# Decode attention with a gated FFN: TensorE's twelve looped rounds as one nest of two loops, with the FFN's transposes behind it

## The chip, the cores and the metric

The kernel runs on one core of one Trainium2 chip. A time is device microseconds of one execution; the median of a few executions is what counts. The engines are named as in the profile: PE (TensorE; PEld is its weight load), DVE (VectorE), ACT (ScalarE), POOL (GpSimd) and SP (SyncE, which here only issues DMAs).

## The reference

Two inputs of 448 numbers (batch B = 2, one token) go through an attention block with a cache of 4096 keys and values for each of 16 heads (width 256), and through a feed-forward net (FFN); a gate mixes the two. All is float32.

```python
g = sigmoid((x * gate_w).sum(-1, keepdims=True))
q = (x @ wq).reshape(B, 1, 16, 256).transpose(0, 2, 1, 3)
scores = einsum("bhqd,bhkd->bhqk", q, k_cache) * 256 ** -0.5
o = einsum("bhqk,bhkd->bhqd", softmax(scores), v_cache)
a = o.transpose(0, 2, 1, 3).reshape(B, 1, 4096) @ wo
h = x @ w1 + b1                  # 448 -> 1792
b = (max(h, 0) ** 2) @ w2 + b2   # 1792 -> 448
out = g * a + (1 - g) * b
```

The two caches are 268 MB of the 290 MB that the kernel reads.

## The kernel before, in words

**Rounds.** The work is cut into 16 rounds. A round is one batch row and two heads: 8.39 MB of keys and 8.39 MB of values. The two heads lie on partitions 0 to 63 and 64 to 127, 64 cache rows of 256 numbers on each partition. Keys have two buffers (`kp[0]`, `kp[1]`, even and odd rounds), values have one (`vp`).

**One round.** DVE multiplies the keys with q, spread over all partitions, and adds up each product row: `times_q` and `row_sums` for one half of the buffer, then the other (together `rest`). `maximum` takes the largest score of each partition on DVE and lets PE turn these into rows (tile `mt`); `softmax` takes the negative maximum of a head on DVE (`nb`) and the exponentials and their sums on ACT (`pw`, `rs`). `values` multiplies `pw` with the values, 32 matmuls on PE into the PSUM bank `po`. `make_q` spreads the q of a later round with a matmul of one picked column (`sel`, written by `pick` on ACT).

**Groups.** Four heads (two batch rows, so four rounds) are a group u. After the fourth round `sums(u)` adds the exponentials' sums over partitions, `norm(u)` makes the factors on DVE, `turn_wide(u)` copies `po` to `shared` on ACT and transposes and scales it on PE, and `project(u)` multiplies it with this group's rows of `wo` into `acc`. Rounds 0 to 11 (`LOOPED`) are groups 0 to 2; the last four rounds have code of their own, with w2 loaded last of all.

**The FFN.** x times w1 goes into the PSUM bank `ph` early on. ACT copies it to `h_sb` (in `shared`), `ffn_turn` transposes it with 28 small matmuls between round 0's softmax and the loops, and `ffn_square` (five DVE instructions: bias, maximum with 0, square, gate) stands on DVE between round 1's `rest` and its `maximum`. Its result `hT` is first used with w2, at the end.

**Order.** Every engine executes its instructions in the order in which the program calls `op`. `Flow.op` works out the semaphore waits from the regions that an instruction reads and writes. SP issues all large loads on one DMA queue, in program order, and each waits for its buffer to come free: `load_k(i + 2)` for `row_sums` of round i, `load_v(i + 1)` for `values` of round i. On PE the four rounds of a group are a loop of the hardware (`Fori`), with the group's end as straight code behind it, three times over. In such a loop waits have to be the same on each pass, so they are tokens: a semaphore that an instruction of another engine raises (`give`) and PE lowers again (`take`).

Of the kernel before, what the change touches and what calls it, by code (L numbers as in the profile page):

```python
# [23 lines left out]
class Flow:  # L24
# [7 lines left out]
    def __init__(self, nc):  # L32
        self.nc = nc
        self.eng = {PE: nc.tensor, ACT: nc.scalar, DVE: nc.vector, POOL: nc.gpsimd, SP: nc.sync}
        self.order = {e: [] for e in self.eng}
        self.ops = {}
        self.know = {e: {} for e in self.eng}
        self.seen = {}
        self.tokens = {}
        self.body, self.at, self.passes = None, 0, 0  # L40

# [4 lines left out]
    def op(self, eng, fn, r=(), w=(), give=None, take=(), dma=None):  # L46
        proc = dma or eng
        looped = eng == PE and self.body is not None
        o = Op(proc, eng, fn, give, looped)
# [38 lines left out]
        if looped:  # L88
            if self.passes == 1:
                self.body.append(o)  # L90
            else:
                first = self.body[self.at]
# [11 lines left out]

    def loop(self):
        self.body, self.passes = [], 0

    def next_pass(self):
        assert self.passes < 2 or self.at == len(self.body)
        self.passes += 1  # L110
        self.at = 0

    def end_loop(self, slot=None):
        assert self.at == len(self.body)
        self.order[PE].append((self.passes, self.body, slot))
        self.body = None

    def emit(self):
# [36 lines left out]
        for eng in (POOL, DVE, ACT, SP, PE):  # L155
            for o in self.order[eng]:
                if isinstance(o, Op):
                    one(o)
                else:
                    passes, body, slot = o  # L160
                    with nc.Fori(0, passes, engines=bass.OrderedEngineSet([TYPES[PE]]),
                                 head_slot=None if slot is None else {TYPES[PE]: slot}):
                        for p in body:
                            one(p)
            if eng == SP:
                nums = sorted(s.num for s in sems.values())
                assert nums == list(range(nums[0], nums[0] + len(nums)))
                nc.sync.sem_clear(range(nums[0], nums[0] + len(nums)))


def gated_mix_kernel(nc, x, k_cache, v_cache, wq, wo, w1, b1, w2, b2, gate_w, out):
# [134 lines left out]
    def vec(fn, r, w, give=None):  # L306
# [12 lines left out]
    vec(lambda: v_.tensor_reduce(m16, ident.rearrange("p (r k) -> p k r", r=4)[:, :4 * HG, :], axis=AX.X, op=ALU.add),  # L319
        ["ident"], ["m16"])  # L320

    xr = start_at[:, 4 * D:].rearrange("b (k r s) -> b k r s", k=XC, s=2)
# [51 lines left out]
    def make_q(i, token=False):  # L374
        c = sel if token else col(i)
        op(PE, mms([(pq[k * PH:(k + 1) * PH, :DH], c.to_broadcast([P, PH]), qs[:, k * DH:(k + 1) * DH], True, True)
                    for k in range(2)]), r=["qs", "sel" if token else "ident"], w=["pq"], take=["q"] if token else ())
        t = q_t[i % 3]
        q_of[i] = t
        op(ACT, lambda: s_.activation(t, pq[:, :DH], AF.Copy), r=["pq"], w=[f"q{i % 3}"])  # L380

    def pick(i):
        c = col(i)
        op(ACT, lambda: s_.activation(sel, c, AF.Copy), r=["ident"], w=["sel"], give="q")

# [6 lines left out]

    h_sb = shared[:2 * B, :F // 2]
    op(PE, times_x(ph, w1_t, D, FB // 2), r=["xT", place(vp, 0, D * F // P)], w=["ph"])
    for k in range(FB // 2):
        op(ACT, lambda k=k: s_.activation(h_sb[:, k * D:(k + 1) * D], ph[32 * k:32 * k + 2 * B, :D], AF.Copy),
           r=["ph"], w=[("shared", k * D, (k + 1) * D)])
    load_k(1)
# [20 lines left out]
    def maximum(i, token=False):  # L419
        s = s_t[i % 2]  # L420
        vec(lambda: v_.tensor_reduce(m, s, axis=AX.X, op=ALU.max), [f"s{i % 2}"], ["m"], give="m" if token else None)
        op(PE, mms([(mt[k * PH:(k + 1) * PH, :PH], m.to_broadcast([P, PH]), ident[:, k * PH:(k + 1) * PH], True, True)
                    for k in range(2)]), r=["m", "ident"], w=["mt"], take=["m"] if token else ())

# [3 lines left out]
    def softmax(i):  # L428
        b, n = rounds[i]
        s, nb, rs, pw = s_t[i % 2], nb_t[i % 2], None, pwt[buf(i)]  # L430
        vec(lambda: v_.tensor_reduce(nb, mt[:, :PH], axis=AX.X, op=ALU.max, negate=True), ["mt"], [f"nb{i % 2}"])  # L431
        u, k = unit_of[2 * n]
        rs = rs_t[u % 2]

        def part(e):
            at = slice(e * PH, (e + 1) * PH)
            c = B * (k + e) + b
            op(ACT, lambda: s_.activation(pw[at, :, 2 * c:2 * c + 2], s[at].rearrange("p (m s) -> p m s", s=2), AF.Exp,  # L438
                                          bias=nb[at], accum_out=rs[at, c:c + 1]),
               r=[f"s{i % 2}", f"nb{i % 2}"], w=[(f"pw{buf(i)}", 2 * c, 2 * c + 2), (f"rs{u % 2}", c, c + 1)],  # L440
               give="pw" if e and i < LOOPED else None)

        part(0)
        part(1)

    def clear(i):
# [4 lines left out]
           w=[("pw0", 2 * (B * (k + e) + b), 2 * (B * (k + e) + b) + 2) for e in range(2)])  # L451

    def sums(u):
        n = B * len(units[u])
        op(PE, mms([(sm[:, :n], ones_pp, rs_t[u % 2][:, :n], True, True)]), r=["ones", f"rs{u % 2}"], w=["sm"])

# [23 lines left out]

    o_w = shared.rearrange("r (s j k p) -> r s j k p", s=2, j=HJ // 2, k=HG)

    def turn_wide(u):
        ptv = sm[:, :HJ * HG * B].rearrange("p (j c) -> p j c", c=HG * B)
        po, rl = po_t[0], rl_t[u % 2]
        pv = po.rearrange("r (s p j) -> r s j p", s=2, j=HJ)
        for lo in range(0, HJ, HJ // 2):
            for s in range(2):
                op(ACT, lambda s=s, lo=lo: s_.activation(o_w[:, s], pv[:, s, lo:lo + HJ // 2].unsqueeze(2).to_broadcast([P, HJ // 2, HG, HP]),  # L489
                                              AF.Copy), r=["po0"], w=[("shared", s * HN // 2, (s + 1) * HN // 2)])  # L490
            ov = o_w.rearrange("r s j k p -> r s j (k p)")
            op(PE, mms([(ptv[:, lo + j, :], ov[:, s, j, :], rl[:, :, s], s == 0, s == 1)
                        for j in range(HJ // 2) for s in range(2)]), r=["shared", f"rl{u % 2}"], w=["sm"])
        if u < NG - 2:
            op(ACT, lambda: s_.activation(po, zero.to_broadcast([P, 512]), AF.Copy), r=["zero"], w=["po0"])
        for k in range(HG):
            at = slice(k * HP, (k + 1) * HP)
            op(ACT, lambda k=k, at=at: s_.activation(oTw[at], ptv[at, :, B * k:B * k + B], AF.Copy), r=["sm"], w=[("oTw", k, k + 1)])  # L498

# [15 lines left out]
    def load_wo(u):  # L515
        if u < NG - 1:
            load(SP, "wo", wo_t, wo_g[u], ["wo"])
        else:
            load(SP, "wo", wo_t.rearrange("p (h k) -> p h k", h=HG), wo_v[:, u * HG:(u + 1) * HG, :], ["wo"])

    def project(u):
        t = wo_t.rearrange("p (j n) -> p j n", j=HJ)
        op(PE, mms([(acc[:B, :D], oTw[:, j, :], t[:, j, :], False, u == NG - 2 and j == HJ - 1) for j in range(HJ)]),
           r=["oTw", "wo"], w=["acc"])

# [42 lines left out]
    softmax(0)  # L568
    pt = ffn_turn()
    make_q(2)  # L570
    pick(3)

    for i in range(LOOPED):
        if i % HG == 0:
            flow.loop()
        flow.next_pass()
        vt = load_v(i, vp)
# [9 lines left out]
        softmax(i + 1)  # L587
        make_q(i + 3, True)
# [101 lines left out]
```

## Time and profile before

| | |
|---|---|
| median of 3 runs | 677.68 us (677.60 to 677.97) |
| the profiled execution | 677.82 us, its span 676.5 us |
| DVE busy | 570.2 us, 84% |
| PE busy | 245.4 us, 36% |
| ACT busy | 42.3 us, 6% |
| read from HBM | 289.56 MB, 428 GB/s over the span |
| share of the 16 DMA engines, SP's queue | 99.3% |

The page lists busy time by engine, 40 equal slices of the span, the DMA queues, and the chain of work that ended last. The timeline lists instructions by their start in us from the span's start. In both, a row of a group gives out<-in by tile name, the shape, the count, busy us and mean ns of one, and behind the bar the idle time before it and what ended it. PE executes each float32 matmul as two, so 32 matmuls of the program are x64 in the trace. The DMA rows count KB of 1024 bytes.

### The profile page before, as it was taken

What the parts mean: (1) busy time and instruction counts of PE and PEld (TensorE: products, weight loads), DVE (VectorE), ACT (ScalarE), POOL (GpSimd) and SP (SyncE); (2) the same over time, 40 slices, a digit from 0 to 9 for tenths busy, and PEclk for the clock granted to TensorE, in tenths of its full rate; (3) what the DMA queues carried; (4) which work ended last, traced back from release to release, by engine and by line L of the source; (5) the groups of instructions that cost most, each with busy time, mean ns of one, the idle gap of its engine ahead of it and who ended that gap; (6) DMA issues with size and microseconds to landing.
All of it is one profiled execution on the core that took longest, in us unless ns stands there. A gap on an engine that the chain in (4) does not pass through costs nothing.

```text
span 676.5 us, 3789 instructions
## 1 busy us (share of the span) xinstructions
PE 245.4 (36%) x1658; PEld 83.3 (12%) x1658; DVE 570.2 (84%) x143; ACT 42.3 (6%) x141; POOL 0.7 (0%) x6
## 2 busy tenths in 40 slices
PE   2522350502305761140505456050411580412476
PEld 1100210100001410010101411010100140100122
DVE  3069999999999895979979896897979899999920
ACT  0001000010100201010000201000010110000000
POOL 0000000000000000000000000000000000000000
PEclk9957585655758577585756678575665765675889
DMA  9999999999999999999999999999999999999997
GB/s 381 426 438 435 435 434 434 434 434 434 434 434 434 419 435 434 434 434 434 434 434 434 457 431 434 434 434 434 430 434 430 401 460 434 434 434 434 392 439 304
DMA packets 7062, 289.71 MB, mean 428 GB/s; under 512 B 902, under 2 KB 1036, under 8 KB 1932
## 3 DMA queue, kind: packets, MB, share of 16 engines
q1 hardware_dynamic: 6880, 289.54, 99.3%
q8 instruction: 8, 0.13, 0.1%
q10 hardware_dynamic: 172, 0.02, 0.0%
q14 instruction: 2, 0.02, 0.0%
HBM read 289.56 MB, written 0.01 MB: 428 GB/s over the span
## 4 chain that ended last, share of the span: by engine, by line
DMA 48%; DVE 31%; PE 3%; SPq 1%; issue 0%; DVEq 0%
DMA kp<-in_A_k_cache_dram 32%; DVE s L409 15%; DVE kp L404 15%; DMA vp<-in_A_v_cache_dram 11%; DMA kp<-in_B_w_dram 5%; PE po L333 3%; SPq L254 1%; PE fin L333 0%; PE mt L333 0%; DVE shared L660 0%; DVEq L147 0%; DVE nb L431 0%
## 5 line engine op out<-in xcount | busy, mean ns | idle before, releaser
L404 DVE TENSOR_TENSOR kp<-kp,q 128x8192 f32<-128x8192 f32 (+2 forms) x34 | 278.2, 8183 | 57.6 <-DMA kp<-in_A_k_cache_dram 57.6
L409 DVE TENSOR_REDUCE s<-kp 128x32 f32<-128x8192 f32 x32 | 278.0, 8686 | 1.1
L333 PE MATMUL po<-vp,pw 128*16 128x512 f32 (+1 forms) x960 | 135.8, 728 | 233.0 <-PEq L145 208.9
L333 PEld LDWEIGHTS po<-vp,pw 128*16 128x16 f32 (+1 forms) x960 | 31.1, 110 | 333.5 <-issue 307.3
L333 PE MATMUL mt<-ident,m 128*64 128x64 f32 x64 | 7.3, 318 | 141.3 <-PEq L145 87.4
L333 PE MATMUL sm<-rl,shared 128*128 128x8 f32 (+1 forms) x112 | 23.6, 347 | 9.2 <-ACT shared L489 8.1
L333 PE MATMUL acc<-wo,oTw 128*2 128x448 f32 x48 | 24.8, 683 | 2.5 <-ACT oTw L498 2.5
L333 PEld LDWEIGHTS sm<-rl,shared 128*128 128x128 f32 x112 | 23.0, 311 | 10.8 <-DVE rl L462 4.6
L450 ACT ACTIVATE pw<-zero 128x128 f32<-128x128 f32 x12 | 3.7, 312 | 325.5 <-PE po L333 325.5
L333 PEld LDWEIGHTS mt<-ident,m 128*64 128x64 f32 x64 | 4.8, 191 | 155.0 <-issue 99.0
L438 ACT ACTIVATE pw<-s,nb 64x64 f32<-64x64 f32 x32 | 11.1, 348 | 169.8 <-DVE nb L431 169.6
L660 DVE COPY shared<-fin 128x112 f32<-128x112 f32 x1 | 0.3, 275 | 20.8 <-PE fin L333 20.8
L333 PE MATMUL ph<-vp,xT 128*4 128x448 f32 x28 | 8.2, 759 | 15.6 <-DMA vp<-in_B_w_dram 15.6
L333 PE MATMUL po<-kp,pw 128*8 128x512 f32 x64 | 9.4, 744 | 8.8 <-DMA kp<-in_A_v_cache_dram 8.8
L333 PE MATMUL pq<-qs,sel 128*64 128x256 f32 x48 | 12.3, 594 | 0.0
L431 DVE TENSOR_REDUCE nb<-mt 128x1 f32<-128x64 f32 x16 | 3.6, 224 | 9.8 <-PE mt L333 9.8
L333 PE MATMUL po<-vp,xT 128*4 128x512 f32 x56 | 8.7, 787 | 4.9 <-DMA vp<-in_A_wq_dram 4.9
L460 DVE RECIPROCAL rc<-sm 128x8 f32<-128x8 f32 (+1 forms) x5 | 1.0, 196 | 7.7 <-PE sm L333 7.7
L380 ACT ACTIVATE q<-pq 128x256 f32<-128x256 f32 x16 | 6.1, 383 | 21.0 <-PE pq L333 20.7
L489 ACT ACTIVATE shared<-po 128x512 f32<-128x512 f32 x12 | 6.5, 591 | 11.4 <-PE sm L333 11.4
L333 PEld LDWEIGHTS acc<-wo,oTw 128*2 128x2 f32 x48 | 4.5, 98 | 20.6 <-issue 17.8
L438 ACT ACTIVATION_READ_ACCUMULATOR pw<-s,nb 64x1 f32 x32 | 5.9, 184 | 0.0
(65 smaller groups left out, 66.2 us busy)
## 6 DMA issues: line engine op xcount, KB each, us to landing
vp<-in_A_wq_dram SPq DMA_DIRECT2D x1, 7168.0 KB, 19.4
wo<-in_A_wo_dram SPq DMA_DIRECT2D x4, 1792.0 KB, 45.2
vp<-in_A_v_cache_dram SPq DMA_DIRECT2D x1, 4096.0 KB, 24.8
vp<-in_B_w_dram SPq DMA_DIRECT2D x1, 3136.0 KB, 18.0
vp<-in_A_v_cache_dram SPq DMA_DIRECT2D x1, 3072.0 KB, 31.7
kp<-in_B_w_dram SPq DMA_DIRECT2D x1, 1344.0 KB, 37.1
vp<-in_A_v_cache_dram SPq DMA_DIRECT2D x1, 1024.0 KB, 33.7
kp<-in_B_w_dram SPq DMA_DIRECT2D x2, 448.0 KB, 33.5
```

What stands on the lines that cost most here:

```text
L254: op(eng, lambda: e.dma_start(dst, src), r=r, w=w, dma=sem, give=give)
L333: i = t_.matmul(out_, lhsT, rhs, start=start, stop=stop, skip_group_check=True)
L380: op(ACT, lambda: s_.activation(t, pq[:, :DH], AF.Copy), r=["pq"], w=[f"q{i % 3}"])
L404: vec(lambda: v_.tensor_tensor(kt, kt, q.unsqueeze(1).to_broadcast([P, hi - lo, DH]), op=ALU.mult), at + [f"q{i % 3}"], at)
L409: vec(lambda: v_.tensor_reduce(s[:, at], rows(t)[:, at, :], axis=AX.X, op=ALU.add), [place(t, half * HALF, (half + 1) * HALF)], [(f"s{i % ...
L431: vec(lambda: v_.tensor_reduce(nb, mt[:, :PH], axis=AX.X, op=ALU.max, negate=True), ["mt"], [f"nb{i % 2}"])
L438: op(ACT, lambda: s_.activation(pw[at, :, 2 * c:2 * c + 2], s[at].rearrange("p (m s) -> p m s", s=2), AF.Exp, bias=nb[at], accum_out=rs[at ...
L450: op(ACT, lambda: s_.activation(at, zero.unsqueeze(2).unsqueeze(3).to_broadcast([P, NK // 2, 2, 2]), AF.Copy), r=["zero"], w=[("pw0", 2 * ...
L460: vec(lambda: v_.reciprocal(c, sm[:, :B * n].rearrange("p (k b) -> p k b", b=B)), ["sm"], ["rc"])
L489: op(ACT, lambda s=s, lo=lo: s_.activation(o_w[:, s], pv[:, s, lo:lo + HJ // 2].unsqueeze(2).to_broadcast([P, HJ // 2, HG, HP]), AF.Copy), ...
L660: vec(lambda: v_.tensor_copy(y4, fin[:, :DQ]), ["fin"], [("shared", 0, DQ)])
```

## The change

PE's three loops of four passes become one nest: an outer loop over the groups 0 to 2, an inner loop over a group's four rounds, and the group's end (`sums`, turn, `project`) as the rest of the outer body. Waits of that rest become tokens too: `turn` and `oT` from ACT, `wo` from the load, and `pick` now gives the `pw` token that `values` takes. Some steps have fewer matmuls. `make_q` and `maximum` have one full-width matmul each in place of two half-width ones (and two half-height copies or reductions behind them). At a group's end DVE itself scales and adds the two column halves of `po` into a tile `o` of 256 columns (`norm_wide`, five instructions where `norm` had three), ACT writes it to `shared` in one instruction of 1024 columns, and PE turns it with 8 matmuls where it had 16. The sums of a group are held in a copy (`rs_w`).

The FFN's turn moves from ahead of the loops to behind them, with `ffn_square` right after it. Its input stays in the PSUM bank `ph` until then, and ACT copies it, twice over, into the tile `wo_t` after the third `project` has read that. It has 14 matmuls of 128 columns for 28 of 64.

```diff
@@ Flow.emit
+                    outer, inner, body, rest, slot = o
+                    with nc.Fori(0, outer, engines=engines, head_slot={TYPES[PE]: slot}):
+                        with nc.Fori(0, inner, engines=engines):
+                            for p in body:
+                                one(p)
+                        for p in rest:
                             one(p)
@@ make_q, pick, maximum
-        op(PE, mms([(pq[k * PH:(k + 1) * PH, :DH], c.to_broadcast([P, PH]), qs[:, k * DH:(k + 1) * DH], True, True)
-                    for k in range(2)]), r=["qs", "sel" if token else "ident"], w=["pq"], take=["q"] if token else ())
+        op(PE, mms([(pq[:, :2 * DH], c.to_broadcast([P, P]), qs, True, True)]), r=["qs", "sel" if token else "ident"], w=["pq"])
...
-        op(ACT, lambda: s_.activation(sel, c, AF.Copy), r=["ident"], w=["sel"], give="q")
+        op(ACT, lambda: s_.activation(sel, c, AF.Copy), r=["ident"], w=["sel"], give="pw")
...
+        op(PE, mms([(mt[:, :P], m.to_broadcast([P, P]), ident, True, True)]), r=["m", "ident"], w=["mt"], take=["m"] if token else ())
@@ the early copies of ph are gone
-    h_sb = shared[:2 * B, :F // 2]
-    for k in range(FB // 2):
-        op(ACT, lambda k=k: s_.activation(h_sb[:, k * D:(k + 1) * D], ph[32 * k:32 * k + 2 * B, :D], AF.Copy),
-           r=["ph"], w=[("shared", k * D, (k + 1) * D)])
@@ a group's end
+    def norm_wide(u):
+        c = rc[:, :HG]
+        po = po_t[0]
+        vec(lambda: v_.reciprocal(c, sm[:, :B * HG].rearrange("p (k b) -> p k b", b=B)), ["sm"], ["rc"])
+        vec(lambda: v_.tensor_tensor(c, c, gP[:, 0, :].unsqueeze(1).to_broadcast([P, HG, B]), op=ALU.mult), ["rc", "gP"], ["rc"])
+        vec(lambda: v_.tensor_tensor(rw, m8, c.rearrange("p k b -> p (k b)"), op=ALU.mult), ["m8", "rc"], ["rw"])
+        vec(lambda: v_.tensor_scalar(o_t, po[:, :DH], eo[:, 0:1], None, op0=ALU.mult), ["po0", "eo"], ["o"])
+        vec(lambda: v_.scalar_tensor_tensor(o_t, po[:, DH:], eo[:, 1:2], o_t, op0=ALU.mult, op1=ALU.add), ["po0", "eo", "o"], ["o"])
 
     def turn_wide(u):
...
+        op(ACT, lambda: s_.activation(o_w, o_t.rearrange("r (p j) -> r j p", j=HJ).unsqueeze(2).to_broadcast([P, HJ, HG, HP]),
+                                      AF.Copy), r=["o"], w=["shared"], give="turn")
+        ov = o_w.rearrange("r j k p -> r j (k p)")
+        op(PE, mms([(ptv[:, j, :], ov[:, j, :], rw, True, True) for j in range(HJ)]), r=["shared", "rw"], w=["sm"], take=["turn"])
@@ the FFN's turn
     def ffn_turn():
-        hv = h_sb.rearrange("r (p c) -> r c p", c=FC)
+        h_sb = wo_t[:2 * B, :F]
+        hv = h_sb.rearrange("r (a k n) -> r k a n", a=2, k=FB // 2)
+        for k in range(FB // 2):
+            op(ACT, lambda k=k: s_.activation(hv[:, k], ph[32 * k:32 * k + 2 * B, :D].unsqueeze(1).to_broadcast([2 * B, 2, D]), AF.Copy),
+               r=["ph"], w=["wo"])
+        hc = h_sb.rearrange("r (m c) -> r c m", c=FC)
         pt = sm[:, :FC * 2 * B].rearrange("p (c r) -> p c r", r=2 * B)
-        op(PE, mms([(pt[a * PH:(a + 1) * PH, c, :], hv[:, c, :], ident[:2 * B, :2 * B], True, True)
-                    for c in range(FC) for a in range(2)]), r=["shared", "ident"], w=["sm"])
+        op(PE, mms([(pt[:, c, :], hc[:, c, :], ident[:2 * B, :2 * B], True, True) for c in range(FC)]), r=["wo", "ident"], w=["sm"])
         return pt
@@ the order of the program
     softmax(0)
-    pt = ffn_turn()
     make_q(2)
     pick(3)
 
+    flow.nest()
     for i in range(LOOPED):
...
         clear(i)
         rest(i + 1, 0, 0)
-        if i == 0:
-            ffn_square(pt)
...
         if i % HG == HG - 1:
+            flow.enter("outer")
             u = i // HG
-            flow.end_loop(16 * u)
             sums(u)
-            norm(u)
+            norm_wide(u)
             turn_wide(u)
             project(u)
+    flow.end_nest(NG - 1, HG, 39)
+    pt = ffn_turn()
+    ffn_square(pt)
 
     i = last - 3
     load_k(i + 2)
```

How this moves instructions, at the places of which the prediction speaks. In the kernel before, DVE has the FFN's five instructions (L560 to L564) between the sums and the maximum of round 1:

```order
L409 TENSOR_REDUCE s1<-kp1 128x32
L560 TENSOR_TENSOR hb<-sm,b1T 64x28 x2
L562 TENSOR_SCALAR hb<-hb 128x28
L563 TENSOR_TENSOR hT<-hb 128x28
L564 TENSOR_TENSOR hT<-hT,gP 128x28
L421 TENSOR_REDUCE m<-s1 128x1
```

They read `sm`, which PE filled ahead of its loops. At the end of the third group, behind round 12's maximum (L421, L431), DVE has the factors (L460 to L462) and then round 13's keys:

```order
L421 TENSOR_REDUCE m<-s0 128x1
L431 TENSOR_REDUCE nb0<-mt 128x1
L460 RECIPROCAL rc<-sm 128x8
L461 TENSOR_TENSOR rc<-rc,gP 128x8
L462 TENSOR_TENSOR rl0<-m16,rc 128x16
```

In the changed kernel (its own line numbers) the same place on DVE holds, between round 12's maximum and round 13's keys (L412 on kp1), the factors, the two instructions that make `o`, and the FFN:

```order
L429 TENSOR_REDUCE m<-s0 128x1
L440 TENSOR_REDUCE nb0<-mt 64x1 x2
L499 RECIPROCAL rc<-sm 128x8
L500 TENSOR_TENSOR rc<-rc,gP 128x8
L501 TENSOR_TENSOR rw<-m8,rc 128x8
L502 TENSOR_SCALAR o<-po0,eo 128x256
L503 SCALAR_TENSOR_TENSOR o<-po0,eo,o 128x256
L582 TENSOR_TENSOR hb<-sm,b1T 64x28 x2
L584 TENSOR_SCALAR hb<-hb 128x28
L585 TENSOR_TENSOR hT<-hb 128x28
L586 TENSOR_TENSOR hT<-hT,gP 128x28
L412 TENSOR_TENSOR kp1<-kp1,q1 128x8192
```

So the FFN's instructions now stand ahead of round 13's products, and what they read is made on PE at that same time. PE's order there, in the changed kernel, from the head of the inner loop (L166; L165 is the outer one) to the FFN's transposes:

```order
L166 UNCONDITIONAL_BRANCH
L344 MATMUL po0<-vp,pw0 16x512 x32
L344 MATMUL mt<-ident,m 128x128
L344 MATMUL pq<-qs,sel 128x512
L166 REGISTER_ALU
L166 COMPARE_AND_BRANCH
L344 MATMUL sm<-rs_w,ones_pp 128x8
L344 MATMUL sm<-rw,shared 128x8 x8
L344 MATMUL acc<-wo,oTw 2x448 x8
L165 REGISTER_ALU
L165 COMPARE_AND_BRANCH
L344 MATMUL sm<-ident,wo 128x4 x14
```

The FFN's 14 transposes (the last row) come behind the third `project` (`acc`), where the kernel before goes from `project` straight to round 13's maximum.

More of the change, by code (lines that the diff above doesn't have):

```diff
@@ L39, in __init__ @@
         self.tokens = {}
-        self.body, self.at, self.passes = None, 0, 0
+        self.parts, self.part, self.at = None, None, 0
     @staticmethod
@@ L47, in op @@
         proc = dma or eng
-        looped = eng == PE and self.body is not None
+        looped = eng == PE and self.part is not None
         o = Op(proc, eng, fn, give, looped)
@@ L88, in op @@
         if looped:
-            if self.passes == 1:
-                self.body.append(o)
+            if self.at is None:
+                self.parts[self.part].append(o)
             else:
-                first = self.body[self.at]
+                first = self.parts[self.part][self.at]
                 assert first.takes == o.takes and not o.waits, (first.takes, o.takes)
@@ L103, in learn, with nest, enter, leave @@
         know[p.proc] = max(know.get(p.proc, 0), p.n)
[L105 to L116, printed above, removed]
+    def nest(self):
+        self.parts = {}
+    def enter(self, part):
+        self.leave()
+        self.part, self.at = part, 0 if part in self.parts else None
+        self.parts.setdefault(part, [])
+    def leave(self):
+        assert self.part is None or self.at in (None, len(self.parts[self.part]))
+        self.part = None
+    def end_nest(self, outer, inner, slot):
+        self.leave()
+        self.order[PE].append((outer, inner, self.parts["inner"], self.parts["outer"], slot))
     def emit(self):
@@ L159, in emit @@
                 else:
[L160 to L163, printed above, removed]
+                    outer, inner, body, rest, slot = o
+                    engines = bass.OrderedEngineSet([TYPES[PE]])
+                    with nc.Fori(0, outer, engines=engines, head_slot={TYPES[PE]: slot}):
[3 more added lines that the diff above has]
+                        for p in rest:
                             one(p)
@@ L220, in gated_mix_kernel @@
     m16 = sb("m16", P, 4 * HG)
+    m8 = sb("m8", P, 2 * HG)
+    rw = sb("rw", P, 2 * HG)
+    o_t = sb("o", P, DH)
+    rs_w = sb("rs_w", P, B * HG)
     xT = sb("xT", P, 2, XC, 2, B)
@@ L320, in gated_mix_kernel @@
         ["ident"], ["m16"])
+    vec(lambda: v_.tensor_reduce(m8, m16.rearrange("p (c s) -> p c s", s=2), axis=AX.X, op=ALU.add), ["m16"], ["m8"])
     xr = start_at[:, 4 * D:].rearrange("b (k r s) -> b k r s", k=XC, s=2)
@@ L375, in make_q @@
         c = sel if token else col(i)
-        op(PE, mms([(pq[k * PH:(k + 1) * PH, :DH], c.to_broadcast([P, PH]), qs[:, k * DH:(k + 1) * DH], True, True)
-                    for k in range(2)]), r=["qs", "sel" if token else "ident"], w=["pq"], take=["q"] if token else ())
+        op(PE, mms([(pq[:, :2 * DH], c.to_broadcast([P, P]), qs, True, True)]), r=["qs", "sel" if token else "ident"], w=["pq"])
         t = q_t[i % 3]
         q_of[i] = t
-        op(ACT, lambda: s_.activation(t, pq[:, :DH], AF.Copy), r=["pq"], w=[f"q{i % 3}"])
+        for k in range(2):
+            at = slice(k * PH, (k + 1) * PH)
+            op(ACT, lambda k=k, at=at: s_.activation(t[at], pq[at, k * DH:(k + 1) * DH], AF.Copy), r=["pq"], w=[(f"q{i % 3}", k, k + 1)])
     def pick(i):
         c = col(i)
-        op(ACT, lambda: s_.activation(sel, c, AF.Copy), r=["ident"], w=["sel"], give="q")
+        op(ACT, lambda: s_.activation(sel, c, AF.Copy), r=["ident"], w=["sel"], give="pw")
     op(PE, times_x(po_t[1], wq_t, QB, NQ // 2), r=["xT", place(vp, 0, D * N // P)], w=["po1"])
@@ L421, in maximum @@
         vec(lambda: v_.tensor_reduce(m, s, axis=AX.X, op=ALU.max), [f"s{i % 2}"], ["m"], give="m" if token else None)
-        op(PE, mms([(mt[k * PH:(k + 1) * PH, :PH], m.to_broadcast([P, PH]), ident[:, k * PH:(k + 1) * PH], True, True)
-                    for k in range(2)]), r=["m", "ident"], w=["mt"], take=["m"] if token else ())
+        op(PE, mms([(mt[:, :P], m.to_broadcast([P, P]), ident, True, True)]), r=["m", "ident"], w=["mt"], take=["m"] if token else ())
     def buf(i):
@@ L430, in softmax @@
         s, nb, rs, pw = s_t[i % 2], nb_t[i % 2], None, pwt[buf(i)]
-        vec(lambda: v_.tensor_reduce(nb, mt[:, :PH], axis=AX.X, op=ALU.max, negate=True), ["mt"], [f"nb{i % 2}"])
+        for k in range(2):
+            at = slice(k * PH, (k + 1) * PH)
+            vec(lambda at=at: v_.tensor_reduce(nb[at], mt[at, at], axis=AX.X, op=ALU.max, negate=True), ["mt"], [(f"nb{i % 2}", at.start, at.stop)])
         u, k = unit_of[2 * n]
-        rs = rs_t[u % 2]
+        rn = u % 2 if u > NG - 2 else 0
+        rs = rs_t[rn]
         def part(e):
@@ L439, in part @@
                                           bias=nb[at], accum_out=rs[at, c:c + 1]),
-               r=[f"s{i % 2}", f"nb{i % 2}"], w=[(f"pw{buf(i)}", 2 * c, 2 * c + 2), (f"rs{u % 2}", c, c + 1)],
-               give="pw" if e and i < LOOPED else None)
+               r=[f"s{i % 2}", (f"nb{i % 2}", e * PH, (e + 1) * PH)], w=[(f"pw{buf(i)}", 2 * c, 2 * c + 2), (f"rs{rn}", c, c + 1)])
         part(0)
@@ L451, in clear, with hold_sums @@
            w=[("pw0", 2 * (B * (k + e) + b), 2 * (B * (k + e) + b) + 2) for e in range(2)])
+    def hold_sums():
+        op(ACT, lambda: s_.activation(rs_w, rs_t[0], AF.Copy), r=["rs0"], w=["rs_w"])
     def sums(u):
         n = B * len(units[u])
-        op(PE, mms([(sm[:, :n], ones_pp, rs_t[u % 2][:, :n], True, True)]), r=["ones", f"rs{u % 2}"], w=["sm"])
+        rs, name = (rs_t[u % 2], f"rs{u % 2}") if u > NG - 2 else (rs_w, "rs_w")
+        op(PE, mms([(sm[:, :n], ones_pp, rs[:, :n], True, True)]), r=["ones", name], w=["sm"])
     def norm(u):
@@ L479, in values @@
         op(PE, mms(calls), r=[f"pw{buf(i)}", place(vt, 2 * lo * DH, 2 * hi * DH)], w=[name], take=["pw", "v"] if token else ())
-    o_w = shared.rearrange("r (s j k p) -> r s j k p", s=2, j=HJ // 2, k=HG)
+    o_w = shared.rearrange("r (j k p) -> r j k p", j=HJ, k=HG)
+    def norm_wide(u):
[6 more added lines that the diff above has]
+        vec(lambda: v_.scalar_tensor_tensor(o_t, po[:, DH:], eo[:, 1:2], o_t, op0=ALU.mult, op1=ALU.add), ["po0", "eo", "o"], ["o"])
@@ L483, in turn_wide @@
     def turn_wide(u):
         ptv = sm[:, :HJ * HG * B].rearrange("p (j c) -> p j c", c=HG * B)
[L485 to L493, printed above, removed]
+        op(ACT, lambda: s_.activation(o_w, o_t.rearrange("r (p j) -> r j p", j=HJ).unsqueeze(2).to_broadcast([P, HJ, HG, HP]),
+                                      AF.Copy), r=["o"], w=["shared"], give="turn")
@@ L494, in turn_wide @@
+        ov = o_w.rearrange("r j k p -> r j (k p)")
+        op(PE, mms([(ptv[:, j, :], ov[:, j, :], rw, True, True) for j in range(HJ)]), r=["shared", "rw"], w=["sm"], take=["turn"])
         if u < NG - 2:
-            op(ACT, lambda: s_.activation(po, zero.to_broadcast([P, 512]), AF.Copy), r=["zero"], w=["po0"])
+            op(ACT, lambda: s_.activation(po_t[0], zero.to_broadcast([P, 512]), AF.Copy), r=["zero"], w=["po0"])
         for k in range(HG):
             at = slice(k * HP, (k + 1) * HP)
-            op(ACT, lambda k=k, at=at: s_.activation(oTw[at], ptv[at, :, B * k:B * k + B], AF.Copy), r=["sm"], w=[("oTw", k, k + 1)])
+            op(ACT, lambda k=k, at=at: s_.activation(oTw[at], ptv[at, :, B * k:B * k + B], AF.Copy), r=["sm"], w=[("oTw", k, k + 1)],
+               give="oT" if k == HG - 1 else None)
@@ L516, in load_wo @@
         if u < NG - 1:
-            load(SP, "wo", wo_t, wo_g[u], ["wo"])
+            load(SP, "wo_given", wo_t, wo_g[u], ["wo"], give="wo")
         else:
@@ L523, in project @@
         op(PE, mms([(acc[:B, :D], oTw[:, j, :], t[:, j, :], False, u == NG - 2 and j == HJ - 1) for j in range(HJ)]),
-           r=["oTw", "wo"], w=["acc"])
+           r=["oTw", "wo"], w=["acc"], take=["oT", "wo"])
     def late(lt, rhs, start=False, stop=False):
@@ L568, in gated_mix_kernel @@
     softmax(0)
-    pt = ffn_turn()
     make_q(2)
     pick(3)
+    flow.nest()
     for i in range(LOOPED):
-        if i % HG == 0:
-            flow.loop()
-        flow.next_pass()
+        flow.enter("inner")
         vt = load_v(i, vp)
@@ L587, in gated_mix_kernel @@
         softmax(i + 1)
+        if (i + 1) % HG == HG - 1:
+            hold_sums()
         make_q(i + 3, True)
```

## The prediction

> **What bounds the kernel now.** I read the page first: the busy shares, the DMA row of the 40 slices and the queues.
>
> ```profile
> PE 245.4 (36%) x1658; PEld 83.3 (12%) x1658; DVE 570.2 (84%) x143; ACT 42.3 (6%) x141; POOL 0.7 (0%) x6
> DMA  9999999999999999999999999999999999999997
> q1 hardware_dynamic: 6880, 289.54, 99.3%
> q8 instruction: 8, 0.13, 0.1%
> ```
>
> SP's queue (q1) fills 99.3% of 16 DMA engines' span, and every slice but the last is at 9. Whatever a compute engine saves is worth nothing here, unless a load is issued so late that the queue runs dry. PE has 64% of its time free. So the question about this change is a single one: does it make some load late?
>
> The chain that ended last, in order of time, shows how the last 150 us hang together (start us, us, what):
>
> ```profile
> 528.44 8.70 DVE s L409
> ...
> 537.16 0.33 SPq L254
> ...
> 537.53 46.46 DMA vp<-in_A_v_cache_dram
> 583.99 0.04 issue
> 584.04 9.31 PE po L333 x64
> 593.34 0.02 issue
> 593.36 29.33 DMA vp<-in_A_v_cache_dram
> ...
> 640.53 32.71 DMA kp<-in_B_w_dram
> ```
>
> The values of round 12, v(12), are issued at 537.53 and land at 583.99; v(13) lands at 593.36 + 29.33 = 622.69. Between the two landings the queue moved the keys k(15) and v(13), so one such load of 8.39 MB takes 38.70 / 2 = 19.35 us, and k(15) landed at 603.34. The last piece of w2 lands at 673.24, and 3.3 us later the span ends.
>
> The timeline round the end of the third group (rounds 8 to 11) in the kernel before shows who waits there:
>
> ```profile
> 537.16 0.33 SPq L254 DMA_DIRECT2D kp<-in_A_k_cache_dram  x1
> 537.53 0.43 SPq L254 DMA_DIRECT2D vp<-in_A_v_cache_dram  x1
> 539.43 0.21 DVE L460 RECIPROCAL rc<-sm 128x8 f32<-128x8 f32 x1 [1.16 <-PE sm L333]
> 539.87 0.18 DVE L462 TENSOR_TENSOR rl<-m,rc 128x16 f32<-128x16 f32 x1
> 540.68 3.49 PEld L333 LDWEIGHTS sm<-rl,shared 128*128 128x128 f32 x16 [1.39 <-DVE rl L462]
> 540.72 3.55 PE L333 MATMUL sm<-rl,shared 128*128 128x8 f32 x16 [1.32 <-ACT shared L489]
> 541.02 8.69 DVE L404 TENSOR_TENSOR kp<-kp,q 128x8192 f32<-128x8192 f32 x1 [0.97 <-DMA kp<-in_A_k_cache_dram]
> 549.12 0.73 ACT L498 ACTIVATE oTw<-sm 32x16 f32<-32x16 f32 x4 [3.67 <-PE sm L333]
> 549.91 8.38 PE L333 MATMUL acc<-wo,oTw 128*2 128x448 f32 x16 [0.82 <-ACT oTw L498]
> 575.78 0.33 SPq L254 DMA_DIRECT2D kp<-in_A_k_cache_dram  x1
> ```
>
> DVE is through with the factors at 540.05, waits 0.97 us for round 13's keys, and starts on them at 541.02. The turn and `project` run on ACT and PE beside it until 558.3, and nobody waits for them. At 575.78 DVE has released `kp[1]` and SP issues k(15), 8.2 us before v(12) lands and the queue would be empty. That 8.2 us is the whole margin.
>
> **The change, part by part.** *Rounds 0 to 11.* Fewer matmuls, one branch more per group and tokens for waits all lie on PE and ACT, which have time. The nearest row is PE's wait between the first group's `project` and the next `values`:
>
> ```profile
> 246.58 2.76 PE L333 MATMUL po<-vp,pw 128*16 128x512 f32 x12 [6.15 <-PEq L145]
> ```
>
> 6.15 us were free there, and the turn now has 16 weight loads for 32. On DVE each group's end gets two instructions of 128x256 and each round one more small reduction. Priced below at 0.75 and about 0.14 us, they lie ahead of a start that waits for keys, or, in the first rounds, delay the issue of loads into a queue that the DMA row shows full. Round 1 loses the FFN's five instructions, about 1 us, in the same place. I cost all of this at nothing; the cover is the full queue. If it were gone, the balance would still be within 1 or 2 us.
>
> *The end of the third group.* Here the change puts a wait into DVE's order. `ffn_square` needs the transposes on PE; they need ACT's copies of `ph` into `wo_t`; those must wait until `project(2)` has read `wo_t`; that needs the turn, and that needs DVE's own `o`. Behind the waiting instruction DVE has all of `rest(13)`, and behind that, on SP, k(15) and everything later. The rows for its length (the landing times are those of the four loads of `wo`; two more of `project`; the last row is the first load of the kernel, 7.34 MB):
>
> ```profile
> L404 DVE TENSOR_TENSOR kp<-kp,q 128x8192 f32<-128x8192 f32 x30 | 260.6, 8685 | 57.6 <-DMA kp<-in_A_k_cache_dram 57.6
> L404 DVE TENSOR_TENSOR kp<-kp,q 128x1024 f32<-128x1024 f32 x2 | 2.4, 1216 | 0.0
> L380 ACT ACTIVATE q<-pq 128x256 f32<-128x256 f32 x16 | 6.1, 383 | 21.0 <-PE pq L333 20.7
> L489 ACT ACTIVATE shared<-po 128x512 f32<-128x512 f32 x12 | 6.5, 591 | 11.4 <-PE sm L333 11.4
> 75.08 3.62 PE L333 MATMUL sm<-ident,shared 4*64 4x4 f32 x56
> 109.97 0.37 DVE L560 TENSOR_TENSOR hb<-sm,b1T 64x28 f32<-64x28 f32 x2
> 110.82 0.19 DVE L564 TENSOR_TENSOR hT<-hT,gP 128x28 f32<-128x28 f32 x1
> DMA to landing us min/median/max: 35.3/45.2/46.5
> 498.82 0.43 SPq L254 DMA_DIRECT2D wo<-in_A_wo_dram  x1
> 231.63 8.80 PE L333 MATMUL acc<-wo,oTw 128*2 128x448 f32 x16 [0.82 <-ACT oTw L498]
> 391.04 7.61 PE L333 MATMUL acc<-wo,oTw 128*2 128x448 f32 x16 [0.82 <-ACT oTw L498]
> vp<-in_A_wq_dram SPq DMA_DIRECT2D x1, 7168.0 KB, 19.4
> ```
>
> Step by step from the reciprocal at 539.43:
>
> 1. `o`: DVE needs 1.04 ns per column and 0.15 us beside (from 1216 ns at 1024 and 8685 at 8192), so 0.42 us for 256 columns. Three small instructions to 540.05, two of these overlapping a little: 540.8.
> 2. ACT's one copy of 1024 columns: 0.81 ns per column and 0.18 us (383 ns at 256, 591 at 512), so 1.0 us: 541.9.
> 3. The turn, 8 matmuls, x16 in the trace, like the first half before: 0.15 us to start and 3.55: 545.6.
> 4. The four copies to `oTw`, 0.73: 546.4. The rows of `wo` have landed by then: issued at 498.82, at most 46.5 us under way, 545.3.
> 5. `project`, 8.38: 554.9.
> 6. Two ACT copies of 896 columns, 0.91 each, a little overlapped: 556.7.
> 7. The FFN's transposes, x28 in the trace. The old ones have the same 1792 columns in x56 and took 3.62. The turn's weight loads, of 128 columns too, took 218 ns each (3.49 / 16), which gives 6.1. The old transposes are the nearer row; with something for the wider load I take 4.2: 560.9.
> 8. `ffn_square`, 109.97 to 111.01, 1.04: about 562.1.
>
> So `rest(13)` starts at 562.1 and not at 541.02, 21.1 us later. k(15) is then issued at 575.78 + 21.1 = 596.9. The queue has only k(14) and v(12), issued at 537 as before, and runs dry when v(12) lands at 583.99. A load into an empty queue needs a start-up: the first one, 7.34 MB, took 19.4 us, of which 16.9 are its bytes at 19.35 us per 8.39 MB, so 2.5 us. k(15) lands at 596.9 + 2.5 + 19.35 = 618.7 and not at 603.34: **15.4 us late**. About 13 of these are an idle queue, the rest its start-up.
>
> ```profile
> 610.88 0.33 SPq L254 DMA_DIRECT2D kp<-in_A_v_cache_dram  x1
> ```
>
> Is any of it made up later? DMA fills the rest of the kernel before (583.99 to 673.24), so there is nothing to catch up with. Is anything worse late next? DVE is 21.1 us behind, DMA only 15.4, so the buffers that DVE releases have 5.7 us less margin. v(14) waits for `rest(14)`: issued at 610.88 before, 11.8 us ahead of v(13)'s landing; 6.1 us of that remain. w2 waits for half of `rest(15)`, which comes before v(15) has landed. So the tail keeps its shape. The sum: 677.82 + 15.4 = 693.2 for the execution that was profiled, which is 0.14 above the median of the runs; I give **693.2**.
>
> Bounds. Low: `project` 7.61, transposes 3.5, `o` and the copies 0.8 us less in all: the start is 18.4 us later, k(15) 12.7 us late, 690.5. High: `project` 8.80, transposes 6.1, 1 us more in copies and waits: about 24.5 us later, 18.8 us late, 696.6.
>
> On step 7 the trace has 218 ns for a load of 128 columns at one place and, late in the kernel, 8 in 1.02 us, 128 ns:
>
> ```profile
> 632.20 1.02 PEld L333 LDWEIGHTS sm<-rl,shared 128*128 128x128 f32 x8 [1.72 <-issue]
> ```
>
> The Trainium skill (TensorE: Matmul & The Clock Gate, LDWEIGHTS) has columns / 1.2 ns, 107 ns for 128 columns: by it the 28 would be 3.0 us and the sum 1.2 us less, 692.0, and the rows of the trace are above that figure in both places.
>
> **The rivals.** *A fetch of instructions at the nest's end.* PE leaves a block that it has gone through twelve times; if the code behind it has to be fetched then, PE's transposes and with them DVE wait longer, and it all lands on the same chain. Small loads that shared the engines with the first large one give a price: the gate's weights were issued at 1.34 and DVE had to wait for them until 9.41.
>
> ```profile
> 1.34 0.25 ACTq L254 DMA_DIRECT2D kp<-in_gate_w_dram  x1
> 9.41 0.61 DVE L354 SCALAR_TENSOR_TENSOR kp<-kp 2x448 f32<-2x448 f32 x1 [2.25 <-DMA kp<-in_gate_w_dram]
> ```
>
> That is 8.1 us: 693.2 + 8.1 = 701.3. Against it: the kernel before also leaves loops, at the end of each group, and PE went from round 12's maximum to the turn with no wait but that for DVE and ACT (0.15 us behind ACT). It decides from the first us of a fetch on. The Trainium skill (Runtime: NRT & Kernel Launch, Instruction fetch mechanics) says that fetching runs ahead in sequence, and that a taken branch whose target is out of the two-page window stalls for a fetch. By that rule leaving the nest is free and the backward branches are what could stall. Those lie ahead of waits like the 6.15 us one.
>
> *The margin holds.* The time would be as before, 677.8, or up to 1 us less by the FFN's instructions in round 1 if, against the full queue, the chain through DVE counted there. The point: k(15) must be issued 2.5 us before 583.99, so `rest(13)` must start by 546.7. For: the queue has 8.2 us in hand, and the FFN's own DVE work is 1 us. Against: `project` alone is 7.61 at its fastest and stands in front of the transposes. It takes an error of 15 us in my chain, or an order on DVE other than the program's.
>
> *The nest isn't one block* and is fetched anew on each pass: eight packets on q8 would become many more, PE's waits in the loops absorb it, and the time stays near 693.
>
> **How the numbers follow.** The forecast, a dry queue behind v(12): 0.83, of which 0.02 is for the third rival. A fetch or another wait on top of it: 0.09. The margin holds: 0.07. Something slower by another way: 0.01. A measurement of this kernel can tell about 0.2%, 1.4 us; the margin's 0.07 I split into 0.03 faster and 0.04 the same. Slower 0.93. The range takes the forecast's bounds with a us below and reaches to the fetch rival's near half: 689.5 to 700.
>
> **What would show it.** In the changed kernel's profile one slice or two between 584 and 600 us have DMA well below 9. DVE has an idle of about 20 us ahead of L582, put down to PE's `sm`, and round 13's products start near 562. k(15) is issued near 597, and the chain runs through the FFN's transposes, `project` and the turn. Before 537 us everything stands where it stood, within 2 us. q8 has fewer than eight packets. I am wrong if DVE's idle ahead of L582 is under 6 us, if DMA stays at 9 there, or if anything before 537 us moved by more than 2.

## The result and the profile after

| | before | after |
|---|---|---|
| median | 677.73 us (6 runs, 677.55 to 677.97) | 698.73 us (6 runs, 698.34 to 698.89) |
| profiled execution, its span | 677.82, 676.5 | 698.89, 697.5 |
| ratio to before | | 1.0309 (95% interval 1.0296 to 1.0323) |

The changed kernel is 21.0 us slower. The same parts of the page, after:

```profile
PE 255.1 (37%) x1518; PEld 82.6 (12%) x1518; DVE 577.2 (83%) x166; ACT 49.4 (7%) x151; POOL 0.7 (0%) x6
DMA  9999999999999999999999999999999992599997
q1 hardware_dynamic: 6880, 289.54, 96.3%
q8 instruction: 5, 0.08, 0.0%
```

The bytes are the same. The DMA row has a hole in slices 33 and 34 of 0 to 39 (a slice is 17.4 us), where both slices were at 9 before. The instruction queue q8 has five packets where it had eight, so the nest was not fetched anew on its passes.

Three stretches of the changed kernel, with the DMA share and GB/s in the last two columns, give the hole's edges (a DMA packet counts in the stretch in which it starts):

```profile
580.00:582.00 2.00, 0.00 (x0) 0.00 (x0) 2.00 (x1) 0.00 (x0) 0.00 (x0) 0.50 0.15 66
582.00:600.00 18.00, 0.00 (x0) 0.00 (x0) 17.97 (x3) 0.00 (x0) 0.00 (x0) 0.50 0.00 0
600.00:602.00 2.00, 0.63 (x2) 0.50 (x2) 1.97 (x3) 0.00 (x0) 0.00 (x0) 0.50 0.00 0
```

For 20 us no packet starts (the last ones of v(12) end at 583.55), while DVE, the third of the engines' busy times, hardly rests. The timeline of the changed kernel round the end of the third group shows what DVE did before that:

```profile
536.58 0.33 SPq L264 DMA_DIRECT2D kp<-in_A_k_cache_dram  x1
539.69 0.21 DVE L499 RECIPROCAL rc<-sm 128x8 f32<-128x8 f32 x1 [1.46 <-PE sm L344]
540.73 0.48 DVE L503 SCALAR_TENSOR_TENSOR o<-po,eo,o 128x256 f32<-128x256 f32 x1
541.25 2.04 ACT L507 ACTIVATE shared<-o 128x1024 f32<-128x1024 f32 x1 [1.02 <-DVE o L503]
543.43 3.55 PE L344 MATMUL sm<-rw,shared 128*128 128x8 f32 x16 [3.78 <-PEq L148]
548.08 8.35 PE L344 MATMUL acc<-wo,oTw 128*2 128x448 f32 x16 [1.09 <-PEq L148]
556.47 1.84 ACT L572 ACTIVATE wo<-ph 4x896 f32<-4x896 f32 x2 [8.71 <-PE acc L344]
558.37 6.97 PE L344 MATMUL sm<-ident,wo 4*128 4x4 f32 x28 [1.94 <-ACT wo L572]
565.38 0.38 DVE L582 TENSOR_TENSOR hb<-sm,b1T 64x28 f32<-64x28 f32 x2 [24.16 <-PE sm L344]
566.34 8.68 DVE L412 TENSOR_TENSOR kp<-kp,q 128x8192 f32<-128x8192 f32 x1
601.09 0.33 SPq L264 DMA_DIRECT2D kp<-in_A_k_cache_dram  x1
```

This is the predicted chain, link by link: DVE waits 24.16 us for PE's transposes, starts on round 13 at 566.34 (541.02 before), and k(15) is issued at 601.09 (575.78 before), 25.3 us late. The chain of waits agrees. It runs through those links, and where it ran over k(15)'s neighbours on the DMA queue before, it now runs through DVE's products and sums without a gap, up to the issue of w2:

```profile
548.08 8.37 PE acc L344 x16
...
556.47 0.91 ACT wo L572
...
558.37 6.99 PE sm L344 x28
...
566.42 8.61 DVE kp L412
...
661.04 33.16 DMA kp<-in_B_w_dram
```

That does not make DVE the bound of the tail. SP issues w2 from 655.40 on, and PE can start on v(14) only at 662.72, so the queue still had v(14) and v(15) to move.

### The profile page after: what moved, and what is told of

It is laid out like the page before. It is cut to its first block, busy times and chain, and to the rows that moved or that the text cites. A ratio compares the mean times of both kernels' runs of the same rounds, so it can differ in the third digit from the quotient of the medians.

```text
span 697.5 us, 3524 instructions
## 1 busy us (share of the span) xinstructions
PE 255.1 (37%) x1518; PEld 82.6 (12%) x1518; DVE 577.2 (83%) x166; ACT 49.4 (7%) x151; POOL 0.7 (0%) x6
## 5 line engine op out<-in xcount | busy, mean ns | idle before, releaser
L412 DVE TENSOR_TENSOR kp<-kp,q 128x8192 f32<-128x8192 f32 (+2 forms) x34 | 278.3, 8184 | 47.9 <-DMA kp<-in_A_k_cache_dram 47.7
L344 PE MATMUL mt<-ident,m 128*128 128x128 f32 x32 | 12.1, 479 | 177.6 <-PEq L148 93.5
L344 PEld LDWEIGHTS mt<-ident,m 128*128 128x128 f32 x32 | 7.8, 303 | 191.3 <-issue 104.3
L344 PE MATMUL pq<-qs,sel 128*128 128x512 f32 x24 | 22.1, 1022 | 0.0
L440 DVE TENSOR_REDUCE nb<-mt 64x1 f32<-64x64 f32 x32 | 7.1, 222 | 13.4 <-PE mt L344 12.9
L344 PE MATMUL po<-kp,pw 128*8 128x512 f32 x64 | 12.6, 959 | 8.6 <-DMA kp<-in_A_v_cache_dram 8.6
L344 PE MATMUL sm<-rw,shared 128*128 128x8 f32 x48 | 10.7, 360 | 11.5 <-PEq L148 11.5
L392 ACT ACTIVATE q<-pq 64x256 f32<-64x256 f32 x32 | 12.1, 378 | 17.8 <-PE pq L344 17.6
L344 PEld LDWEIGHTS sm<-rw,shared 128*128 128x128 f32 x48 | 10.5, 331 | 11.7 <-issue 11.7
L344 PE MATMUL sm<-ident,wo 4*128 4x4 f32 x28 | 7.0, 380 | 1.9 <-ACT wo L572 1.9
L344 PEld LDWEIGHTS sm<-ident,wo 4*128 4x128 f32 x28 | 6.9, 336 | 2.8 <-ACT wo L572 2.8
L344 PEld LDWEIGHTS acc<-wo,oTw 128*2 128x2 f32 x48 | 4.5, 96 | 20.4 <-issue 20.4
```

The lines of the kernel that those rows point to most:

```text
L344: i = t_.matmul(out_, lhsT, rhs, start=start, stop=stop, skip_group_check=True)
L392: op(ACT, lambda k=k, at=at: s_.activation(t[at], pq[at, k * DH:(k + 1) * DH], AF.Copy), r=["pq"], w=[(f"q{i % 3}", k, k + 1)])
L412: vec(lambda: v_.tensor_tensor(kt, kt, q.unsqueeze(1).to_broadcast([P, hi - lo, DH]), op=ALU.mult), at + [f"q{i % 3}"], at)
L440: vec(lambda at=at: v_.tensor_reduce(nb[at], mt[at, at], axis=AX.X, op=ALU.max, negate=True), ["mt"], [(f"nb{i % 2}", at.start, at.stop)])
```

## Experiments

The theory: DVE's wait for the FFN makes k(15) late, the queue runs dry, and nothing else costs anything. The rival: the nest itself (tokens, narrower steps, a fetch at its end) costs part of it, above all the 5.6 us by which the 21.0 exceed the predicted 15.4.

**square_late.** The nest and the late transposes stay; DVE's five instructions move to a place where they find their input ready.

```diff
     pt = ffn_turn()
-    ffn_square(pt)
...
     softmax(i + 1)
+    ffn_square(pt)
     times_q(i + 2, 0, LEAD, J)
```

> The changed kernel, with the FFN's five DVE instructions moved behind round 13's softmax; the nest and the transposes behind it stay. If DVE's wait is the whole cause: round 13's products start near 541 us, no slice between 580 and 602 us is dry, and the time is that of the kernel before, 677.7 (677 to 678.5). If the nest, the tokens or a fetch at its end cost the part that the prediction lacked (5.6 us): 682 to 684.

Measured: 678.00 us against 678.02 for the kernel before on the same chip, ratio 1.0003 (0.9993 to 1.0012). The timeline of this run at the two places:

```profile
541.40 8.68 DVE L412 TENSOR_TENSOR kp<-kp,q 128x8192 f32<-128x8192 f32 x1
558.30 6.97 PE L344 MATMUL sm<-ident,wo 4*128 4x4 f32 x28 [1.94 <-ACT wo L572]
576.15 0.33 SPq L264 DMA_DIRECT2D kp<-in_A_k_cache_dram  x1
577.92 0.38 DVE L582 TENSOR_TENSOR hb<-sm,b1T 64x28 f32<-64x28 f32 x2
```

PE does the FFN's transposes at 558.30 as in the changed kernel, DVE does not wait for them, and the loss is gone. So the nest, the tokens, the narrower turn and the late transposes together cost nothing that can be measured. They gain nothing either: DMA is the bound, and this version ties with the kernel before.

**move_only.** The other half: the kernel before with its three loops, the FFN's turn, in its new form, and its square moved behind them.

```diff
-    pt = ffn_turn()
     make_q(2)
...
-        if i == 0:
-            ffn_square(pt)
...
             project(u)
+    pt = ffn_turn()
+    ffn_square(pt)
```

> The kernel before, three loops as they were, with only the FFN's turn and square moved behind the loops in their new form. DVE's wait as cause: the turn of the kernel before ends project at 558.3, 1.85 us later than in the changed kernel, so round 13 starts 27 us late and the time is 22.5 to 23 us above the kernel before: 700.5. The nest as cause of any part: less than the changed kernel's 698.7.

Measured: 700.83 us, ratio 1.0341 (1.0324 to 1.0358), even a little slower than the changed kernel. DVE's wait ahead of the FFN is 26.67 us here, for the turn in two halves takes longer:

```profile
566.46 0.38 DVE L560 TENSOR_TENSOR hb<-sm,b1T 64x28 f32<-64x28 f32 x2 [26.67 <-PE sm L333]
```

**idle5, idle10, idle25.** The kernel before with nothing but one useless DVE instruction behind the third group's factors, in three lengths: the loss as a function of the delay, without FFN or nest.

```diff
             project(u)
+    idle = sb("idle", P, 49)
+    vec(lambda: v_.tensor_reduce(idle, qs.unsqueeze(1).to_broadcast([P, 49, QB]), axis=AX.X, op=ALU.max), ["qs"], ["idle"])
```

(11 and 20 in place of 49 for the shorter ones.)

> The kernel before with one extra DVE instruction behind the third group's factors: a maximum over q read 11 times, 5632 columns, 6.0 us by the rows of L404, which makes round 13 start 5 us late. Nothing else changes. With a cover of 5.7 us: no loss, 677.7. With 4.3: 0.7 us, 678.4.

> The same with 10240 columns, 10.8 us: round 13 starts 9.9 us late. With a cover of 5.7 us: 4.2 us lost, 681.9. With 4.3: 5.6 us lost, 683.3.

> The same with 25088 columns, 26.3 us: round 13 starts 25.3 us late, as in the changed kernel, without nest, FFN move or new turn. If DVE's late start is the whole cause: 698.7 as the changed kernel, 21 us lost. If the nest or the narrower steps cost anything: less than that by so much. By the cover of 5.7 us: 697.3.

Measured, against 677.91 for the kernel before: 678.60, 683.23 and 698.34, so 0.7, 5.3 and 20.4 us. The 0.7 is loose, for the ten runs of idle5 lie between 677.91 and 680.57; its k(15) is issued at 580.47, 4.7 us late. One row of idle10's timeline, and four of idle25's:

```profile
585.33 0.33 SPq L254 DMA_DIRECT2D kp<-in_A_k_cache_dram  x1
```


```profile
539.84 26.28 DVE L599 TENSOR_REDUCE idle<-qs 128x49 f32<-128x25088 f32 x1
600.78 0.33 SPq L254 DMA_DIRECT2D kp<-in_A_k_cache_dram  x1
642.00 9.43 PE L333 MATMUL po<-vp,pw 128*8 128x512 f32 x64 [5.36 <-DMA vp<-in_A_v_cache_dram]
693.79 0.93 PE L333 MATMUL fin<-kp,hT 128*2 128x112 f32 x24 [0.32 <-DMA kp<-in_B_w_dram]
```

From idle10 to idle25 k(15) is issued 15.45 us later, and the profiled executions (682.88 and 698.38) differ by 15.5: beyond the cover each us late is a us lost. A delay alone, with the loops and the FFN where they were, gives 698.34; the changed kernel with k(15) 0.3 us later has 698.73. The rival, that the nest itself costs part of it, has nothing left to explain.

**square_half.** The changed kernel with the five instructions between the halves of round 13's `rest`.

```diff
-    ffn_square(pt)
...
-    rest(i + 1, 0, 0)
+    times_q(i + 1, 0, 0, J)
+    row_sums(i + 1, 0)
+    ffn_square(pt)
+    times_q(i + 1, 1, 0, J)
+    row_sums(i + 1, 1)
```

> The changed kernel with the five DVE instructions between the two halves of round 13's rest. The first half ends at 558.7, DVE waits for PE until 565.4, and k(15) is issued near 583.8, 8.0 us late. By the cover that the prediction used (8.2 us to the landing of v(12), less 2.5 of start-up, 5.7): 677.7 + 2.3 = 680.0. By the cover that the changed kernel's own loss gives (25.3 late, 21.0 lost, so 4.3): 677.7 + 3.7 = 681.4.

Measured: 681.53 us against 678.02, 3.5 us lost, ratio 1.0055 (1.0038 to 1.0071). Its timeline has k(15) 8.15 us late:

```profile
583.93 0.33 SPq L264 DMA_DIRECT2D kp<-in_A_k_cache_dram  x1
```

The smaller of the two covers in the expectation, 4.3, fits; where the difference lies is worked out below.

**old_turn_form.** The changed kernel with the FFN's transposes in the form of the kernel before, at the new place.

```diff
-        h_sb = wo_t[:2 * B, :F]
+        h_sb = wo_t[:2 * B, :F // 2]
...
-        op(PE, mms([(pt[:, c, :], hc[:, c, :], ident[:2 * B, :2 * B], True, True) for c in range(FC)]), r=["wo", "ident"], w=["sm"])
+        op(PE, mms([(pt[a * PH:(a + 1) * PH, c, :], hv[:, c, :], ident[:2 * B, :2 * B], True, True)
+                    for c in range(FC) for a in range(2)]), r=["wo", "ident"], w=["sm"])
```

> The changed kernel with the FFN's transposes in their old form at the new place: 28 matmuls of 64 columns, and ACT copies of 448 columns instead of 896. If the old row (3.62 us for x56) holds here and the 14 of 128 columns cost 6.97 because two halves of 64 columns overlap and one load of 128 does not: transposes 3.6, copies 1.1 instead of 1.84, so 4.1 us less: 694.6. If the 6.97 comes from PE's clock at this place: transposes near 7, 0.8 us less, 697.9.

Measured: 695.36 us against 678.02, ratio 1.0257 (1.0240 to 1.0274), 3.4 us below the changed kernel. From this run's timeline:

```profile
558.01 3.62 PE L344 MATMUL sm<-ident,wo 4*64 4x4 f32 x56 [1.19 <-ACT wo L571]
597.38 0.33 SPq L264 DMA_DIRECT2D kp<-in_A_k_cache_dram  x1
```

Twice as many instructions, half the time: 3.62 us as in the kernel before, against 6.97. At the clocks granted here it is the form that costs. The stretches of these instructions, in this run, in the changed kernel and in the kernel before, have the granted clock in the third column from the end:

```profile
558.00:561.60 3.60, 3.59 (x56) 3.53 (x56) 0.00 (x0) 0.00 (x0) 0.00 (x0) 0.71 0.76 328
```

```profile
558.40:565.30 6.90, 6.90 (x28) 6.85 (x28) 0.00 (x0) 0.00 (x0) 0.00 (x0) 0.57 1.03 446
```

```profile
75.10:78.70 3.60, 3.60 (x60) 3.58 (x60) 3.51 (x2) 0.87 (x4) 0.00 (x0) 0.50 1.30 564
```

The form of 64 columns took 3.62 us at 0.71 and at 0.50 alike, the wide one 6.97 at 0.57. Loads of 128 columns do differ where the clock does: 218 ns each in the turn at 0.50, and 128 ns each at 632.20 in the kernel before, at 1.00. What the wide form would take at 1.00 no run here shows.

**copy_in_rows.** The changed kernel with `o` in the order in which ACT reads it.

```diff
-        vec(lambda: v_.tensor_scalar(o_t, po[:, :DH], eo[:, 0:1], None, op0=ALU.mult), ["po0", "eo"], ["o"])
+        ot = o_t.rearrange("r (j p) -> r p j", j=HJ)
+        pe, pd = (po[:, k * DH:(k + 1) * DH].rearrange("r (p j) -> r p j", j=HJ) for k in range(2))
+        vec(lambda: v_.tensor_scalar(ot, pe, eo[:, 0:1], None, op0=ALU.mult), ["po0", "eo"], ["o"])
...
-        op(ACT, lambda: s_.activation(o_w, o_t.rearrange("r (p j) -> r j p", j=HJ).unsqueeze(2).to_broadcast([P, HJ, HG, HP]),
+        op(ACT, lambda: s_.activation(o_w, o_t.rearrange("r (j p) -> r j p", j=HJ).unsqueeze(2).to_broadcast([P, HJ, HG, HP]),
```

> The changed kernel with DVE writing o in the order in which ACT reads it, so that ACT's copy of 1024 columns reads neighbouring columns and not every eighth. If the stride in SBUF makes that copy 2.04 us where the rows gave 1.0: it takes 1.0 and the time is 1.0 us less, 697.7, if DVE's two instructions keep their 0.48 us. If not: 698.7 and the copy stays at 2.04.

Measured: 698.18 us, 0.55 less than the median of the changed kernel, whose runs are other ones; that is too little to rest on. The rows of the groups are plain, of this run first and then of the changed kernel:

```profile
L509 ACT ACTIVATE shared<-o 128x1024 f32<-128x1024 f32 x3 | 3.2, 1057 | 3.6 <-DVE o L505 3.6
L505 DVE SCALAR_TENSOR_TENSOR o<-po,eo,o 128x256 f32<-128x256 f32 x3 | 1.9, 647 | 0.1
```

```profile
L507 ACT ACTIVATE shared<-o 128x1024 f32<-128x1024 f32 x3 | 6.2, 2078 | 2.6 <-DVE o L503 2.6
L503 DVE SCALAR_TENSOR_TENSOR o<-po,eo,o 128x256 f32<-128x256 f32 x3 | 1.5, 484 | 0.1
```

ACT's copy falls from 2.08 to 1.06 us, and each of DVE's two instructions grows by 0.16.

## Why the prediction was right, and where it was off

The mechanism, its place and its sign held. The size was off: 693.2 was forecast, and 698.73 lies above the forecast's own high bound of 696.6. It lies in the range because the range was stretched towards the fetch rival, which did not happen; that part is luck. (The low bound is off in itself: 0.77 us less in `project`, 0.7 in the transposes and 0.8 in the rest take the 21.1 us to 18.8 and not to 18.4.) Point by point:

- *Rounds 0 to 11 cost nothing*: right. k(14) is issued at 536.58 (537.16 before), and square_late ties with the kernel before.
- *DVE's wait*: right in kind, 4.2 us too short. `rest(13)` was to start at 562.1 and started at 566.34. Step 2, ACT's copy, was sized at 1.0 us by rows of copies out of PSUM and took 2.04; copy_in_rows gives the price of 1.0 back. Step 7, the transposes, was sized at 4.2, nearer to the old row than to the turn's weight loads, and took 6.97. The turn's row, 218 ns per load of 128 columns, was the near one (249 ns measured), and old_turn_form shows why the other was not. Step 7 had its high bound at 6.1, so that bound was too low as well. The 107 ns of the Trainium skill for 128 columns (TensorE: Matmul & The Clock Gate, LDWEIGHTS) was further off still. Steps 5, 6 and 8 came out within 0.1 us. The 0.4 us that are left of the 4.2 are a reciprocal at 539.69 in place of 539.43, and tenths in between.
- *The cover of 8.2 us and a start-up of 2.5*: right by landings, 1.0 us too much for the time. In the changed kernel k(15) was issued at 601.09 and v(13) had landed when PE started on it, at 642.28; take off two loads of 19.35 and 2.5 us are left. idle25 has 2.5 from its rows above.

```profile
642.28 9.90 PE L344 MATMUL po<-vp,pw 128*8 128x512 f32 x64 [4.55 <-DMA vp<-in_A_v_cache_dram]
```

A landing is the end of the slowest of 16 DMA engines, while the work runs out on each engine by itself. Each engine closes a load with a packet of 4 bytes. By the DMA packets of the two traces, these closing packets end at (us; average of the 16 engines, in brackets the first and the last):

| load | before | changed kernel | later on average |
|---|---|---|---|
| v(12) | 582.37 (581.66 to 583.56) | 581.82 (581.31 to 583.55) | |
| k(15) | 601.72 (601.00 to 602.91) | 622.26 (621.93 to 622.52) | 20.54 |
| v(13) | 621.07 (620.36 to 622.26) | 641.66 (641.37 to 641.90) | 20.59 |
| v(14) | 640.52 (639.70 to 641.61) | 661.16 (660.86 to 662.12) | 20.64 |

On average an engine of the kernel before ends v(12) 1.6 us ahead of the landing at 583.99, and the start-up in the changed kernel is 622.26 - 19.35 - 601.09 = 1.8 us. So the cover was 582.37 - 575.78 - 1.8 = 4.8 us and not 5.7: this term of the sum was mis-sized too. idle10 and idle25 give 4.8 in the same way: k(15) is issued 9.55 and 25.00 us late there and ends 4.80 and 20.25 us late on average.

- *The tail keeps its shape*: right, though the landings hide it. From v(13)'s landing to w2's last piece the kernel before takes 50.55 us, the changed one 694.20 - 642.24 = 51.96, and idle25 693.75 - 641.97 = 51.8, as if 1.4 us were lost in the tail. But on average k(15), v(13) and v(14) are late by nearly the same 20.6 us. About 1.0 of the 1.4 us comes from where the stretch begins: behind the dry spell the engines end v(13) within 0.5 us of each other, before within 1.9, so the last of them, the landing, is only 19.55 us late. The other 0.4 us lie at the end, where w2's last piece lands 20.96 us late; why it is later than the average stays open.

Together 4.2 us of DVE's start, 1.0 of the cover and 0.4 at the end make the 5.6 us that the forecast lacked. *The fetch at the nest's end*, the rival above the forecast, did not happen: PE's only wait ahead of the transposes is 1.94 us for ACT's copies. This agrees with the Trainium skill's rule that fetching runs ahead in sequence (Runtime: NRT & Kernel Launch, Instruction fetch mechanics); whether a branch out of the window stalls no run here shows.

## What to carry to other kernels

In a kernel whose DMA queue is always full, ask of every moved instruction what stands behind it on its own engine and which load that releases: five DVE instructions, 1 us in all, cost 21, by standing in line ahead of a buffer's release with their input not ready. Find the cover first, the time from the issue of the next load to the end of what is queued, less a start-up. Take it on the average DMA engine and not by the landing, which is the slowest engine's: 4.8 us and not 5.7 here. Below the cover a delay costs next to nothing (idle5: 4.7 us late, 0.7 lost), above it each microsecond counts in full (idle10 to idle25). When a producer moves, move its consumer on an in-order engine to where the input is sure to be there; here that alone gave the 21 us back.

## What the runs showed that was not expected

- Loading 128 columns for a 4-row transpose took 249 ns (6.97 us for x28, granted clock 0.57); as two loads of 64 columns into the two halves of the output's partitions it took 129 ns for the pair (3.62 for x56), in the same place. Fewer, wider matmuls were the slower form.
- ACT copied 1024 columns from SBUF in 1.06 us when neighbouring columns were read, and in 2.08 when every eighth was. DVE, which then wrote in that order and read PSUM by neighbours as before, paid 0.16 us per instruction of 256 columns.
- In a queue that had run dry, v(13) landed 2.5 us later than the issue of k(15) and two loads of 19.35 us add up to, in the changed kernel and in idle25; on the average engine the start-up was 1.8 us.
- The dry spell brought the 16 DMA engines into step: they end v(13) within 0.5 us of each other in the changed kernel and within 1.9 us before. So v(13)'s landing, the end of the slowest engine, moved by 1 us less than the average engine did.
